# Another step order for the attention stage, and the range test of the softmax sums split in two

## The chip, the cores and the metric

The kernel runs on one core of a Trainium2 chip. The metric is device time in microseconds (us) of one execution; lower is better. Three runs of the kernel before gave 255.69, 255.74 and 256.41 us, median 255.74 us. The profile is one further execution, with a time of its own.

## The reference

Two branches work on the same 2048 x 512 input and are summed with it:

```python
xn = layernorm(x)                                  # 2048 tokens, 512 features
# A: 32 heads of width 16, causal window of 256 tokens
q, k, v = split(xn @ wqkv)
p = softmax(where(0 <= i - j < 256, q k^T / 4, -1e9))
A = (p v) @ wo
# B: gated MLP with spatial mixing
z = gelu(xn @ w_in)                                # 1376 wide, two halves of 688
g = w_sp @ layernorm(z[:, 688:]) + b_sp            # w_sp is 2048 x 2048
B = (z[:, :688] * g) @ w_out
out = x + A + B
```

All inputs and the output are bf16.

## The kernel before, in words

The kernel has a first stage (layernorm, `z`, most of q, k and v) and an attention stage, in which the attention, the spatial mixing and both output projections are interleaved. Nothing schedules at run time or at build time: every engine takes its instructions in the order in which the program issues them, and in the attention stage that order is the string `ORDER`, one token per step, read by the loop at the end of the kernel. A step issues work on several engines, so moving a step moves its work in all their queues.

The steps:

- `q4` and the numbers behind it: matmuls of 512 columns (L161) of the last four q/k/v projections; here they are tiles of v, which VectorE casts into `v_y` (L168).
- `S`: two score tiles. TensorE writes them into PSUM (`score_mm`, L761), ScalarE takes the exponential (L840), and GpSimd masks the window's edges with `affine_select` (L855) once both halves of a set are there. `B`, `A` and `T` are steps of three tiles, of which VectorE casts the third to bf16 (L838) ahead of its exponential; they also open (`B`, `T`) and close (`A`, `T`) an output tile `fo`.
- `D`: the corner blocks of a unit pair: 32 small score matmuls, two exponentials (L790). `d`: VectorE multiplies those with a mask (L862).
- `p`: the product with v of one of the 32 units (L727, 56 matmuls), followed on VectorE by the transposition `ot` (L734). `n`: VectorE normalizes one unit: a reciprocal into `r_all` (L740), a multiplication (`on`, L742) and a transposition (`oT`, L750).
- `g`: matmuls of 344 columns of the spatial mixing (L588), 16 to a tile `gf`; `g7 ... 9` is such a tile in two parts. VectorE then adds the bias and multiplies with `z1` into `u` (L602), and SyncE issues the transposing DMA of `u` and the load of a later `wspT`.
- `y`: matmuls of the output tile that is open (L662). `f`: those of an output tile on its own (L680, L687). At its end VectorE adds the input (`xo`, L627) and a DMA stores the result.

Two kinds of PSUM buffer couple the engines. The score tiles are three buffers (`ps_s`), so a score step waits until the exponentials of the tiles three earlier are through. All of `q`, `g`, `p`, `y` and `f` share two banks (`x_tile`), which alternate; while an output tile is open it holds one of them, and every `gf` takes the other.

The reciprocals of all softmax sums stay in `r_all`, 512 columns. After the last unit is normalized, `check_sums` tests them against a range with a `tensor_scalar` (L873) and a `scalar_tensor_tensor` with an accumulator (L874), and a DMA turns the 128 counts into one row (L879). Ahead of the last addition of `xo`, VectorE takes that row's minimum (`least_sum`, L886), then writes a flag (L892), which every engine loads; a slower path with a maximum follows only if a sum is out of range, which does not happen with these inputs.

Of the kernel before, what the change touches and what calls it, by code (L numbers as in the profile page):

```python
# [8 lines left out]
P = 128  # L9
BF = mybir.dt.bfloat16  # L10
F32 = mybir.dt.float32
ACT = mybir.ActivationFunctionType
ALU = mybir.AluOpType

S_TOK = 2048
D = 512
# [9 lines left out]
NG = 4  # L26
NJ = NB // 2
SM_SCALE = DH ** -0.5
LN_EPS = 1e-5
R_LOW = 2.0 ** -60  # L30
R_HIGH = 2.0 ** 40
# [11 lines left out]


ORDER = """
S q4 q2 S 2 q4 S q4 g7 D 9 S g10 S d 6 p S g5 n 11 D p p S p g7 D 5 n 3 d 1 g3 n 4 B y1 1 n y1 2
y1 3 y1 1 y1 2 A y3 g3 y1 5 d 2 B 5 y4 1 y2 A y1 g3 y1 2 y1 11 S p p D g12 S 4 n n g6 S 10 S p p
S g5 n 3 n 8 B y5 g1 y1 1 d y1 2 A 2 y1 5 y1 5 D p p D g4 n d 12 B n y2 g1 y1 1 y1 1 y1 3 A y1 1
y1 4 y1 1 y1 4 S p p S g8 n 6 d 2 B y4 g3 y1 1 n 3 A 1 y1 3 y3 5 D p p S g4 n 4 d 8 B y3 n g1 y1
3 y1 2 y1 A 1 y1 5 y2 4 D p p D g2 n 11 n 3 B y3 g3 d y1 1 y1 2 A 3 y2 1 y1 2 y1 4 S p p D g5 n  # L50
8 d 3 B y6 p A y2 d g11 y1 1 S 4 p n S p g6 n D 10 S p g6 n n 5 B y2 1 y1 3 y1 1 y1 d y4 T y8 n
y1 A g16 S p p D n g2 n 13 B y2 1 y4 d y3 T y9 A g16 D p p S g12 D d 4 g6 n S 8 n 2 S p p S g10
D n 4 n 2 f6 S 3 d 1 g7 S 9 S p p S g4 d 9 S n 3 g11 n 5 p p n f7 n 3 f10 f10 f10
"""


# [16 lines left out]
def kernel(  # L73
# [12 lines left out]
    nc = tc.nc  # L86
# [25 lines left out]
    r_all = pers.tile([P, NJ * NG, 16], F32, name="r_all")  # L112
# [63 lines left out]
    with ExitStack() as actx:  # L176
# [52 lines left out]
        for w in WARM:  # L229
# [11 lines left out]
            out=hmask[:],  # L241
# [4 lines left out]
        for m, off, old, new in ((maskY, 0, PAD, 0), (maskD, -PAD, 0, PAD)):  # L246
            nc.gpsimd.memset(m[:], 1.0)
            nc.gpsimd.affine_select(
                out=m[:, old : old + PAD], in_=m[:, old : old + PAD], pattern=[[-1, PAD]],
# [3 lines left out]
                out=m[:, new : new + PAD], in_=m[:, new : new + PAD], pattern=[[1, PAD]],  # L253
# [151 lines left out]
        def z_stats(n):  # L405
            if n % 2 == 0:
                zmv[n // 2] = sm.tile([P, 4, 2], F32, name="zmv")
            mvt = zmv[n // 2]
            st = sm.tile([P, 2, nc.vector.BN_STATS_DIM], F32, name="st2")
            for j in range(2):  # L410
                nc.vector.bn_stats(out=st[:, j, :], in_=z2n[:, n, j * HALF : (j + 1) * HALF])
            nc.vector.bn_aggr(out=mvt[:, n % 2, :], in_=st[:])
            if n % 2 == 1:
                return rstd(mvt, 2)
            return None
# [9 lines left out]
        for n in range(2):  # L425
# [6 lines left out]
            out=maskC[:, 0, :], in0=maskD[:, 0:PAD], in1=maskD[:, PAD:P], op=ALU.add  # L432
        )
        nc.vector.tensor_scalar(
            out=maskC[:, 1, :], in0=maskC[:, 0, :], scalar1=-1.0, scalar2=1.0,
            op0=ALU.mult, op1=ALU.add,
# [18 lines left out]
        for n in range(NB):  # L455
            b, j = divmod(n, 4)
# [25 lines left out]
            if n >= 1:  # L482
                r = z_stats(n - 1)
# [20 lines left out]
            if n % 2 == 1 and n >= 3:  # L504
                r = z_rs[n - 2]
# [4 lines left out]
            if n == NB - 1:  # L510
                r = z_stats(n)
# [11 lines left out]
    ep = ctx.enter_context(tc.tile_pool(name="ep", bufs=4))  # L523
# [6 lines left out]
    def late():  # L530
        if not late_pool:
            assert not work["q"]
            pq_ctx.close()
            late_pool.append(
                late_ctx.enter_context(tc.tile_pool(name="late", bufs=1, side="right"))
            )
            for i in range(2):
                vh = late_pool[0].tile([P, 4, VROW], BF, name=f"vh{i}")
                nc.gpsimd.memset(vh[PAD:P, 0:2, :], 0.0)
                nc.gpsimd.memset(vh[0:PAD, 2:4, :], 0.0)  # L540
                v_half.append(vh)
        return late_pool[0]
# [151 lines left out]
    E = {}  # L694
    ED = {}
    turned = {}
    later = []
# [39 lines left out]
    def normalize(J, G):  # L737
        ot = turned.pop((J, G))
        rsum = r_all[:, J * NG + G, :]
        nc.vector.reciprocal(out=rsum, in_=ot[:, :, DH])  # L740
        on = late().tile([P, 8, 32], BF, name="on", bufs=2)
        nc.vector.tensor_tensor(  # L742
            out=on[:].rearrange("p b (e d) -> p e b d", e=2),
            in0=ot[:].rearrange("p (e b) j -> p e b j", e=2)[:, :, :, 0:DH],
            in1=rsum.rearrange("p (e b) -> p e b", e=2).unsqueeze(3).to_broadcast([P, 2, 8, DH]),
            op=ALU.mult,
        )
        if G == 0:
            oTs[J] = late().tile([P, NC, 256], BF, name="oT", bufs=3)
        nc.vector.transpose(  # L750
            out=oTs[J][:, G, :], in_=on[:].rearrange("p b j -> p (b j)")
        )
# [55 lines left out]
    def do_slots(n, shut=False, open_=False):  # L808
        some = [slots.pop(0) for _ in range(n)]
        tiles = [ps_s.tile([P, 2, 512], F32, name="S", tag="S") for _ in range(n)]  # L810
        mms = []
        for (J, G, kind, h), S in zip(some, tiles):
            if kind == "P" and h == 0:
                E[(J, G)] = ep.tile([P, 8, 512], BF, name="E")
            if (J, G, kind, h) == (0, 2, "Q", 0):
                load_half(1)
            mms.append(list(slot_mms(J, G, kind, h, S)))
        if n == 3:
            h = some[1][3]
            score_mm(*mms[0].pop(0))  # L820
            if shut:
                rest_mm(half[0], 2 * h, False)
            if open_:
                new = half_open()
                rest_mm(new, 2 * h + 1, True)
            turns = [mms[0:1], mms[1:3]]
        else:
            turns = [mms]
        for turn in turns:
            for k in range(0, max(len(m) for m in turn), 2):  # L830
                for m in turn:
                    for args in m[k : k + 2]:
                        score_mm(*args)
        for i, ((J, G, kind, h), S) in enumerate(zip(some, tiles)):
            b0 = 4 * (kind == "Q") + 2 * h
            part, src = E[(J, G)][:, b0 : b0 + 2, :], S[:]
            if i == 2:
                nc.vector.tensor_copy(out=part, in_=src)  # L838
                src = part
            nc.scalar.activation(out=part, in_=src, func=ACT.Exp, scale=SM_SCALE)  # L840
            if h == 1:
                mask_set(J, G, kind)
        if shut:
            half_end()
# [15 lines left out]
    def mask_corners(J, G):  # L860
        v, mask = ED[(J, G // 2)][:], maskC[:, int(J == 0), :]
        nc.vector.tensor_tensor(  # L862
            out=v, in0=v, in1=mask.unsqueeze(1).to_broadcast([P, 32, PAD]), op=ALU.mult,
        )

    rows = []

    def check_sums():
        assert not (later or units)
        r = r_all[:].rearrange("p a b -> p (a b)")  # L870
        ok = ep.tile([P, 512], BF, name="ok", tag="E")
        low = ep.tile([P, 1], F32, name="low", tag="E")
        nc.vector.tensor_scalar(out=ok[:], in0=r, scalar1=R_LOW, scalar2=None, op0=ALU.is_ge)  # L873
        nc.vector.scalar_tensor_tensor(  # L874
            out=ok[:], in0=r, scalar=R_HIGH, in1=ok[:], op0=ALU.is_le, op1=ALU.mult,
            accum_out=low[:],
        )
        row = ep.tile([P, P], F32, name="row", tag="E")
        nc.sync.dma_start(out=row[0:1, :], in_=low[:])  # L879
        rows.append(row)  # L880
# [186 lines left out]
    units = [(J, G) for J in range(NJ) for G in range(NG)]  # L1067
# [6 lines left out]
    for step in ORDER.split():  # L1074
        if step in "STABCH":
            n = 2 if step == "S" else 1 if step == "H" else 3
            do_slots(n, step in "TA", step in "TB")
        elif step == "D":
            do_corners(*corners.pop(0))
        elif step == "d":  # L1080
            mask_corners(*masks.pop(0))
        elif step == "p":
            pv(*units.pop(0))
        elif step == "n":
            normalize(*later.pop(0))
        elif step[0] == "y":
            for _ in range(int(step[1:])):
                half_mm()
        else:
            if step[0] in work:  # L1090
                assert left == 0
                item = work[step[0]].pop(0)
                left, unit = (NFC + NC, f_work(*item)) if step[0] == "f" else item
                step = step[1:]
            for _ in range(int(step)):
                next(unit)
                left -= 1
            if left == 0:
                assert next(unit, None) is None
# [34 lines left out]
```

## Time and profile before

| | value |
|---|---|
| median of three runs | 255.74 us |
| profiled execution, time and span | 255.79 us, 254.0 us |
| first score matmul of the attention stage | 83.23 us |
| last matmul issued / last instruction on data | 250.21 us / 251.22 us |
| TensorE, VectorE, ScalarE, GpSimd busy | 97%, 79%, 77%, 41% of the span |

The span runs from the first to the last instruction of the trace; 1.8 us of the profiled execution's time lie outside it. Matmuls overlap in TensorE's pipeline, so their durations in the tables are longer than the time from one to the next: a matmul of 344 columns lasts 310 ns, and the next one starts 146 ns after it. The sums below therefore go by starts.

### The profile page before, as it was taken

Reading aid. Unit: us, or ns where it says so; the run is one execution under the profiler, and the core shown is the slowest. Engines: PE = TensorE matmul, PEld = TensorE weight load, DVE = VectorE, ACT = ScalarE, POOL = GpSimd, SP = SyncE. Lnnn points to the kernel's source line nnn. Section 1 sums busy time; section 2 is a strip of 40 time slices with the busy share of each in tenths; the row PEclk is TensorE's granted clock in tenths of the full one; section 3 lists DMA queues with packets and bytes.
Section 4 is the critical chain, followed back from the end, with each engine's and each line's share of the span. In section 5 each row is a group of like instructions: output and inputs, shape, how many; then the busy total and the mean of one; then the engine's idle time right before and its main releaser. Section 6 shows DMA issues by size and latency. Waiting matters only on the chain.

```text
span 254.0 us, 8684 instructions
## 1 busy us (share of the span) xinstructions
PE 247.7 (97%) x3712; PEld 141.3 (56%) x3712; DVE 200.1 (79%) x434; ACT 195.6 (77%) x234; POOL 105.3 (41%) x165
## 2 busy tenths in 40 slices
PE   7899999999999999999999999999999999999994
PEld 3555555555555356546557556566565464664653
DVE  7699977875657659985698898887998989684883
ACT  3756567556546998898989989889898899998900
POOL 3221211210010387575464465626484547543710
PEclk9999999999999999999999999999999999999999
DMA  6899722018400128646567717569184557675232
GB/s 198 291 252 195 195 54 31 1 41 104 105 1 0 44 46 122 143 124 137 54 86 181 131 44 189 50 157 157 38 168 41 138 77 126 117 101 125 36 54 69
DMA packets 67162, 26.82 MB, mean 106 GB/s; under 512 B 57040, under 2 KB 65584, under 8 KB 67120
## 3 DMA queue, kind: packets, MB, share of 16 engines
q1 hardware_dynamic: 66400, 25.50, 52.4%
q10 hardware_dynamic: 720, 0.73, 0.9%
q8 instruction: 30, 0.49, 0.9%
q14 instruction: 12, 0.10, 0.1%
HBM read 8.46 MB, written 2.10 MB: 42 GB/s over the span
## 4 chain that ended last, share of the span: by engine, by line
PE 92%; DMA 3%; DVE 2%; ACT 1%; issue 1%; SPq 0%; DVEq 0%
PE gf L588 31%; PE zp L370 14%; PE S L761 11%; PE fo L662 10%; PE o L727 9%; PE pj_o L143 6%; PE pj_f L143 5%; PE pj_o L161 3%; PE pj_f L161 2%; DMA w_in_sb<-in_B_w_in_dram 2%; DMA row<-low 1%; DVE xo L627 1%; PE fo L680 1%; PE zo L370 0%; PE fo L687 0%
## 5 line engine op out<-in xcount | busy, mean ns | idle before, releaser
L855 POOL TENSOR_SCALAR_AFFINE_SELECT E<-E 128x512 bf16<-128x512 bf16 x124 | 86.3, 721 | 68.0 <-ACT E L840 64.8
L840 ACT ACTIVATE E<-S 128x1024 bf16<-128x1024 f32 x102 | 97.6, 1027 | 9.1 <-PE S L761 9.0
L588 PE MATMUL gf<-z2n,wspT 128*128 128x344 bf16 x512 | 88.4, 310 | 0.0
L588 PEld LDWEIGHTS <-wspT 128*128 128x128 bf16 x512 | 47.4, 98 | 30.9 <-issue 5.9
L302 POOL TENSOR_TENSOR rs<-ve,mhalf 128x2 f32<-128x2 f32 (+1 forms) x18 | 12.1, 670 | 68.2 <-DVE ve L299 67.6
L370 PE MATMUL zp<-w_in_sb,xnT 128*128 128x344 bf16 x224 | 36.9, 309 | 0.1
L761 PE MATMUL S<-qpad,kT 32*64 32x128 bf16 (+2 forms) x848 | 32.0, 259 | 0.2 <-ACT E L840 0.2
L790 ACT ACTIVATE ED<-S 128x1024 bf16<-128x1024 f32 x30 | 29.1, 1024 | 1.6 <-PE S L761 1.5
L370 PEld LDWEIGHTS <-xnT 128*128 128x128 bf16 x224 | 21.6, 98 | 14.6 <-ACT xnT L361 0.7
L602 DVE SCALAR_TENSOR_TENSOR u<-gf,b_all,z 128x344 bf16<-128x344 f32 (+3 forms) x50 | 20.4, 438 | 11.7 <-PE gf L588 11.5
L734 DVE STREAM_TRANSPOSE ot<-o 128x512 f32<-128x512 f32 x32 | 22.5, 714 | 7.8 <-PE o L727 7.6
L838 DVE CAST E<-S 128x1024 bf16<-128x1024 f32 x22 | 26.7, 1213 | 2.2 <-PE S L761 2.2
L840 ACT ACTIVATE E<-E 128x1024 bf16<-128x1024 bf16 x22 | 23.4, 1063 | 0.8 <-DVE E L838 0.6
L727 PE MATMUL o<-E,v_y 128*32 128x128 bf16 (+1 forms) x736 | 23.5, 239 | 0.2
L761 PEld LDWEIGHTS <-kT 32*64 32x64 bf16 (+1 forms) x848 | 12.9, 99 | 18.6 <-issue 16.4
L727 PE MATMUL o<-ED,vh 128*32 128x64 bf16 x960 | 21.2, 193 | 0.0
L154 DVE TENSOR_SCALAR qpad<-qt,hmask 128x512 bf16<-128x512 bf16 x32 | 9.7, 348 | 13.6 <-ACT qt L152 13.6
L143 PEld LDWEIGHTS <-wqkv 128*128 128x128 bf16 x128 | 12.5, 98 | 12.8 <-DMA xnT<-xt 0.3
L862 DVE TENSOR_TENSOR ED<-ED,maskC 128x2048 bf16<-128x2048 bf16 x15 | 19.2, 1278 | 0.0
L378 ACT ACTIVATE z<-zp 128x688 bf16<-128x688 f32 x14 | 10.4, 743 | 10.9 <-PE zp L370 10.9
L143 PE MATMUL pj_o<-xnT,wqkv 128*128 128x512 bf16 x72 | 18.5, 379 | 0.0
L378 ACT ACTIVATE z2n<-zp 128x688 bf16<-128x688 f32 x14 | 10.4, 743 | 10.1 <-PE zp L370 10.1
(88 smaller groups left out, 306.7 us busy)
## 6 DMA issues: line engine op xcount, KB each, us to landing
vh<-v_y SPq DMA_DIRECT2D x16, 140.0 KB, 4.4
xo<-in_A_x_dram SPq DMA_DIRECT2D x16, 128.0 KB, 2.9
out_dram<-xo SPq DMA_DIRECT2D x15, 128.0 KB, 2.0
wqkv<-in_A_wqkv_dram SPq DMA_DIRECT2D x1, 1536.0 KB, 8.7
xt<-in_A_x_dram SPq DMA_DIRECT2D x2, 512.0 KB, 3.9
w_in_sb<-in_B_w_in_dram SPq DMA_DIRECT2D x5, 172.0 KB, 5.5
w_out_sb<-in_B_w_out_dram SPq DMA_DIRECT2D x1, 640.0 KB
w_in_sb<-in_B_w_in_dram ACTq DMA_DIRECT2D x3, 172.0 KB, 6.0
```

The costliest lines, as they stand in the source:

```text
L143: nc.tensor.matmul(pt[:], lhsT=wqkv[:, c, w0 : w0 + P], rhs=xnT[:, c, t0 : t0 + 512], start=(c == 0), stop=(c == NC - 1),)
L370: nc.tensor.matmul(out, lhsT=src[:, c, t0 : t0 + P], rhs=w_in_sb[:, c, f0 : f0 + HALF], start=(c == 0), stop=(c == NC - 1),)
L378: nc.scalar.activation(out=dst.rearrange("p (j f) -> p j f", j=2), in_=zp[:, :, 0:HALF], func=ACT.Gelu_apprx_tanh, scale=rsx[n] if n < 2 e ...
L588: nc.tensor.matmul(gf[:, 0:HALF], lhsT=wspT[t][:, c, :], rhs=z2n[:, c, j * HALF : (j + 1) * HALF], start=(c == 0), stop=(c == NB - 1),)
L662: nc.tensor.matmul(h["fo"][:], lhsT=lhsT, rhs=rhs, start=False, stop=(h["jobs"] == 2 and h["pos"] == NFH))
L727: nc.tensor.matmul(o[32 * s : 32 * s + 32, c0 + r0 : c0 + r0 + n], lhsT=v[:, m, h * VW : h * VW + 32], rhs=rhs(s), start=(i == 0), stop=(i ...
L734: nc.vector.transpose(out=ot[:].rearrange("p b j -> p (b j)"), in_=o[:])
L761: nc.tensor.matmul(out, lhsT=kT[32 * s : 32 * s + 32, g, k0 : k0 + nk], rhs=qpad[J // 2][32 * s : 32 * s + 32, g, :, qs - q00 : qs - q00 + ...
L790: nc.scalar.activation(out=Ed[:, 16 * i : 16 * i + 16, :], in_=S[i][:].rearrange("p b (x q) -> p (b x) q", q=PAD), func=ACT.Exp, scale=SM_ ...
L838: nc.vector.tensor_copy(out=part, in_=src)
L840: nc.scalar.activation(out=part, in_=src, func=ACT.Exp, scale=SM_SCALE)
L855: nc.gpsimd.affine_select(out=cells[:, :, k, :], in_=cells[:, :, k, :], pattern=pattern, compare_op=op, fill=0.0, base=base, channel_multi ...
```

## The change

`ORDER` is replaced. It has the same steps in the same numbers, plus one `c`; their places differ from the third token on. The new step `c` calls `test_sums`, which tests the part of `r_all` that has been normalized so far (28 units, 448 columns). `check_sums` tests the remaining four units (64 columns) at its old place, adds the two counts, and sends the sum by the same DMA. The limit that the flag compares with is the same.

```diff
 ORDER = """
-S q4 q2 S 2 q4 S q4 g7 D 9 S g10 S d 6 p S g5 n 11 D p p S p g7 D 5 n 3 d 1 g3 n 4 B y1 1 n y1 2
-y1 3 y1 1 y1 2 A y3 g3 y1 5 d 2 B 5 y4 1 y2 A y1 g3 y1 2 y1 11 S p p D g12 S 4 n n g6 S 10 S p p
-S g5 n 3 n 8 B y5 g1 y1 1 d y1 2 A 2 y1 5 y1 5 D p p D g4 n d 12 B n y2 g1 y1 1 y1 1 y1 3 A y1 1
-y1 4 y1 1 y1 4 S p p S g8 n 6 d 2 B y4 g3 y1 1 n 3 A 1 y1 3 y3 5 D p p S g4 n 4 d 8 B y3 n g1 y1
-3 y1 2 y1 A 1 y1 5 y2 4 D p p D g2 n 11 n 3 B y3 g3 d y1 1 y1 2 A 3 y2 1 y1 2 y1 4 S p p D g5 n
-8 d 3 B y6 p A y2 d g11 y1 1 S 4 p n S p g6 n D 10 S p g6 n n 5 B y2 1 y1 3 y1 1 y1 d y4 T y8 n
-y1 A g16 S p p D n g2 n 13 B y2 1 y4 d y3 T y9 A g16 D p p S g12 D d 4 g6 n S 8 n 2 S p p S g10
-D n 4 n 2 f6 S 3 d 1 g7 S 9 S p p S g4 d 9 S n 3 g11 n 5 p p n f7 n 3 f10 f10 f10
+S q4 q4 q1 S 3 q4 S g8 D 8 g2 S 4 d 6 S 4 p S g12 n 4 p D p n p D g8 n 1 S 7 g4 n 5 B 2 y1 3 y1
+2 y2 d y3 g3 A 4 y2 9 B y2 g1 y1 7 y1 A 2 y5 6 S p p D g4 d 1 n 6 S 5 g4 S 1 n 1 d 10 S p p S g2
+n 2 n 12 B y6 g3 y1 A 1 y1 8 y1 4 D p p D g6 n 4 d 6 B y3 g1 y2 n 2 y1 2 y1 A 1 y1 5 y1 5 S p p
+S g9 n 2 n 5 B y3 g1 d y1 1 y1 1 y1 1 A 1 y2 7 y1 4 D p p S g1 n 6 n 9 B y2 g3 d y1 1 y3 A 1 y1
+2 y2 9 D p p D g5 n 7 n 4 B y2 g6 d y4 A 2 y1 1 y1 3 y1 4 S p p D g5 d 1 n 10 B y6 p A y2 g8 y1
+3 S d 5 p S n p g3 n 4 D 9 S p d g9 n 3 B 3 y2 1 y4 n y3 T n y9 A g16 S p p D g3 n 8 n 4 B 1 y7
+d y2 T y9 A g16 D p p D g1 n 7 d 5 S 3 g4 d 3 S 8 n 1 S p p S n g11 S 5 g6 n c 4 D 6 f2 S 3 d 5
+S p p S g10 S 3 n 3 g11 n 5 p n p n f10 f10 f10 f10
 """
...
+    def test_sums():
+        n0, n1 = sum(tested), NJ * NG - len(units) - len(later)
+        r = r_all[:, n0:n1, :].rearrange("p a b -> p (a b)")
+        ok = late().tile([P, 512], BF, name="ok", tag="ot", bufs=3)
+        if not tested:
+            tested_sums.append(late().tile([P, 2], F32, name="ok_sums"))
+        nc.vector.tensor_scalar(
+            out=ok[:, 0 : r.shape[-1]], in0=r, scalar1=R_LOW, scalar2=None, op0=ALU.is_ge
+        )
+        nc.vector.scalar_tensor_tensor(
+            out=ok[:, 0 : r.shape[-1]], in0=r, scalar=R_HIGH, in1=ok[:, 0 : r.shape[-1]],
+            op0=ALU.is_le, op1=ALU.mult,
+            accum_out=tested_sums[0][:, len(tested) : len(tested) + 1],
+        )
+        tested.append(n1 - n0)
...
     def check_sums():
         assert not (later or units)
-        r = r_all[:].rearrange("p a b -> p (a b)")
...
+        test_sums()
+        sums = tested_sums[0]
+        low = late().tile([P, 1], F32, name="low_sum")
+        nc.vector.tensor_tensor(out=low[:], in0=sums[:, 0:1], in1=sums[:, 1:2], op=ALU.add)
         row = ep.tile([P, P], F32, name="row", tag="E")
         nc.sync.dma_start(out=row[0:1, :], in_=low[:])
         rows.append(row)
...
+        elif step == "c":
+            test_sums()
```

## Prediction

> **What bounds the kernel now.** I read the page first, then the waits, then the timeline of both ends of the attention stage.
>
> ```profile
> PE 247.7 (97%) x3712; PEld 141.3 (56%) x3712; DVE 200.1 (79%) x434; ACT 195.6 (77%) x234; POOL 105.3 (41%) x165
> PE 92%; DMA 3%; DVE 2%; ACT 1%; issue 1%; SPq 0%; DVEq 0%
> ```
>
> TensorE is busy all the time and carries 92% of the chain that ended last. The waits show who holds whom:
>
> ```profile
> PEld L761 <- issue: 16.4, 52, 0.5
> ACT E L840 <- PE S L761: 9.0, 15, 0.8
> PEld L727 <- DVE xo L627: 1.2, 4, 0.4
> PE S L761 <- ACT E L840: 0.2, 1, 0.2
> ```
>
> ScalarE waits 9.0 us for scores, TensorE waits hardly ever for exponentials. The 16.4 us are no wait for another engine: they lie where matmuls of another tile form begin. From starts in the timeline, a `g` matmul costs 0.146 us, a `q`, `y` or `f` 0.216, an `S` 0.33, a `B` or `A` 0.54, a `D` 0.36, a full `p` 0.68, and each change from 128-row matmuls to score or `p` steps about 0.10, always the same within 0.02. So the stage is this sum plus what TensorE waits. Both orders have the same steps and, counted in the strings, 139 changes of form: the sum, 165 us, does not move. Only the waits and the two ends can.
>
> The front, PE, ACT and DVE:
>
> ```profile
> 83.23 0.40 PE L761 MATMUL S<-qpad,kT 32*128 32x512 bf16 x4
> 83.56 1.47 PE L161 MATMUL pj_f<-wqkv,xnT 128*128 128x512 bf16 x6
> 84.96 0.39 PE L761 MATMUL S<-qpad,kT 32*128 32x512 bf16 x2
> 85.53 0.39 PE L761 MATMUL S<-qpad,kT 32*128 32x512 bf16 x2 [0.19 <-ACT E L840]
> 87.26 0.49 PE L761 MATMUL S<-qpad,kT 32*128 32x256 bf16 x8
> ...
> 83.07 1.28 ACT L516 ACT_TABLE_LOAD   x1
> 84.48 5.58 ACT L840 ACTIVATE E<-S 128x1024 bf16<-128x1024 f32 x6
> ...
> 84.75 0.69 DVE L168 CAST v_y<-pj_f 128x512 bf16<-128x512 f32 x1
> ```
>
> The second `S` is cut in two: its second tile needs the buffer of the first exponential, which starts only after the table load. TensorE stands 0.57 us (84.96 to 85.53). The third `S` takes 0.43 instead of 0.33, another 0.10.
>
> The end:
>
> ```profile
> 247.31 0.41 DVE L873 TENSOR_SCALAR ok<-r_all 128x512 bf16<-128x512 f32 x1
> 247.85 0.69 DVE L874 SCALAR_TENSOR_TENSOR ok<-r_all,ok 128x512 bf16<-128x512 f32 x1
> 248.72 0.53 SPq L879 DMA_DIRECT2D row<-low  x1
> 249.88 0.60 PE L687 MATMUL fo<-wo_sb,oT 128*128 128x256 bf16 x4
> 250.68 0.28 DVE L886 TENSOR_REDUCE low<-row 1x1 f32<-1x128 f32 x1 [0.83 <-DMA row<-low]
> 250.88 0.40 DVE L627 TENSOR_TENSOR xo<-fo,xo 128x256 bf16<-128x256 f32 x1
> 251.21 0.13 DVE L892 TENSOR_SCALAR flag<-low 1x1 int32<-1x1 f32 x1
> ```
>
> The last addition stands behind `least_sum`, which waits for the row's DMA (1.93 us after its issue). The last matmul ends at 250.48, and the addition could follow within 0.05 us, as the one before did (matmuls to 248.79 + 0.60 = 249.39, addition at 249.43). It starts at 250.88: 0.35 lost.
>
> **The front, step by step.** Nine `q` instead of six stand ahead of the second `S`. The third group of four `q` wants the bank that the first used, and VectorE empties that from 84.75 to 85.44, behind two normalizations; with 0.06 to release, 85.50. TensorE is there at 83.56 + 8 x 0.216 = 85.29: a new wait of 0.21. One `q` and a change of form later, 85.81, comes the second `S`; its buffer was free at 85.53. The third `S` comes at 85.81 + 0.33 + 7 x 0.216 + 0.10 = 87.75, its buffers free at 87.31. `D` comes at 87.75 + 0.33 + 8 x 0.146 + 0.10 = 89.35; its second buffer is that of the fifth exponential, 88.20 + 1.05 = 89.25: 0.10 to spare, and as little in the next three `S`. So 0.57 + 0.10 go and 0.21 comes: 0.46. What then becomes late is the third `p`. In the old order it reads its last mask at 99.12; the exponentials for it end at 97.63, GpSimd's two selections take 1.27, so that mask is ready at about 98.96. TensorE will be 0.4 earlier; the exponentials only 0.2 to 0.3, what ScalarE idles at 89.90 to 90.19. A wait between 0 and 0.23; I take 0.08, since the old margin was 0.16. Front: **0.38 gained**, between 0.15 and 0.53.
>
> A page speaks against this part. The Trainium skill, "ScalarE: Activation LUTs", section "What ACT_TABLE_LOAD costs", adds a drain of 1.38 us to a load of 1.28; by it, as an estimate, the first exponential would start so much later that the longer cover of nine `q` would not do either. The trace disagrees: the load takes 1.28, and the first exponential starts 0.13 after its end.
>
> **The middle.** The old order has three waits past 100 us, 0.26 in all; the longest, 0.16, is a `p` at 187.04 behind `xo`, itself behind a `d` of 1.68 us (184.71). The new order puts that `d` ahead of the block, so this one goes. New tight places: in `n 7 n 4 B y2 g6` and `n 2 n 5 B y3 g1` two `n` (1.09 each) are queued on VectorE shortly ahead of the emptying of `gf`, and while an output tile is open the next `gf` needs that very bank; I take 0.05 each, at most 0.4. In `3 d 5 S p p` the addition of `xo` is queued behind a `d` (1.18 to 1.68), and the second `p` needs its bank; 0.10, between 0 and 0.3. Middle: **0.05 gained**, between 0.85 lost and 0.26 gained. The step `c` costs VectorE at most 0.41 + 0.69 + 0.08; behind it is queued the emptying of a `gf` that ends ten `g` and a `D` later, 10 x 0.146 + 0.36 + 0.10 = 1.9 us, so I cost it at nothing (without that cover, up to 1.2). SyncE's queue moves along: a `wspT` lands 5.4 us after its issue, the issue comes 1.3 after that of `uT`, and its tile is two further on, 8 us later at the tightest place, early on, in either order; nothing there.
>
> **The end.** After the last `p` the new order has `n` ahead of it and only full `f` behind: the same matmuls in the same order. On VectorE `ot`, `n`, `ot`, `n` closes the gap of 0.22 ahead of the second `ot` (243.94), and the addition of the first `f` starts 0.30 earlier. The tests shrink from 512 to 64 columns. By rows of that size (a 48-column L602 0.26, a 16-column cast 0.17) I take 0.19 and 0.25 for 0.41 and 0.69, and the new addition of two counts costs 0.15 plus a wait of 0.1. The row is issued 0.30 + 0.22 + 0.44 - 0.25 = 0.7 us earlier and lands near 249.95; `least_sum` runs from 249.98 to 250.26, in VectorE's idle time ahead of the last addition. That then follows its matmuls at 250.53 instead of 250.88, and the flag, the last store and the closing semaphores follow it: **0.36 gained**. A landing up to 0.3 later still hides; past that the gain shrinks one for one.
>
> **Sum.** 255.79 (the profiled execution, span 254.0 and 1.8 around it) - 0.38 - 0.05 - 0.36 = 255.00. The median stands 0.05 below the profiled execution: **254.95 us**.
>
> **Rivals.**
>
> (1) TensorE's lead is handed back. ScalarE computes 150 of the 157 us between its first and last exponential, so a lead of 0.4 us may meet buffers and masks that are no earlier. For it: margins of 0.1 in the first ten steps. Against it: ScalarE's own waits for scores, 9 us, mean it is ahead for most of the stage. Only the end's gain is left: 255.74 - 0.36 = 255.4. Chance 0.2.
>
> (2) Slower: VectorE is late at the bank changes. In the blocks from `B` to `A` the new order often has two `y` between `B` and the next `gf`, where the old one had up to five. From the last `g` matmul to that `gf` TensorE needs 0.146 + 0.10 + 0.54 + 2 x 0.216 = 1.22; VectorE starts 0.36 after that matmul's start and needs 0.70 and 0.06 to release: 1.12. Whatever delays it more than 0.1 is a wait. A `d` took 1.68 instead of 1.18 while GpSimd selected, an `on` 1.54 instead of 0.43. The Trainium skill, "GPSIMD Engine Reference", section "Specifications", says that both engines share an interface to SBUF, with contention for instructions with two SBUF inputs; the two rows agree. Half a microsecond in each of five blocks is 2.5: 254.95 + 2.5 = 257.4. It decides from 0.3 a block on. Against it: the old order has the same lengthened rows and lost 0.26 by them. Chance 0.1.
>
> (3) More than that: the old middle waits go, no new ones come, the front keeps 0.53. 255.74 - 0.26 - 0.53 - 0.36 = 254.6. Chance 0.15.
>
> (4) The table load hides more than its row shows, and ScalarE starts later behind the new first steps, by as much as a load (1.28): the second `S` would wait for 86.82 instead of coming at 85.81, 255.95. This is the rule above as a mechanism; the trace shows 0.13, so 0.02.
>
> **How the numbers follow.** My forecast has 0.53. About 0.3% (0.77 us, below 254.97) is what a measurement can tell from no change; the forecast lies on that line. Faster: 0.35 of its 0.53 and all of (3), 0.50. Same: the rest of it, (1) and (4), 0.40. Slower: 0.10. The range takes in (3) below and (1) above with the middle's bounds: 254.4 to 255.6.
>
> **What would show it.** Right: the second `S` in one piece near 85.8 behind a `q` that starts at 85.5; the row's DMA 0.7 earlier against the last matmul, and no gap ahead of the last `xo`. Wrong: TensorE gaps ahead of `S`, `D` or the first four `p` (1), ahead of `gf` inside the blocks (2), or a first exponential later than 84.5 (4).

## The result, and the profile after

The changed kernel takes 257.0 us (median of 18 runs, 255.9 to 258.1) beside 255.79 for the kernel before on the same chip (18 runs, 255.03 to 256.44): ratio 1.0046, 95% interval 1.0033 to 1.0059. It is slower; the forecast of 254.95 and its range of 254.4 to 255.6 are missed. The profiled execution took 257.9 us, with a span of 256.1.

The page, engines and chain:

```profile
PE 247.4 (97%) x3691; PEld 141.3 (55%) x3712; DVE 203.0 (79%) x438; ACT 195.6 (76%) x234; POOL 107.0 (42%) x165
...
PE 91%; DVE 3%; ACT 2%; POOL 1%; issue 1%; POOLq 0%
```

TensorE's work is the same (21 matmul records are missing here), and its share of the chain is smaller. The waits say where:

```profile
PEld L761 <- issue: 16.5, 50, 0.6
...
ACT E L840 <- PE S L761: 9.6, 14, 1.3
...
PEld L727 <- DVE u L602: 1.8, 1, 1.8
PE o L727 <- DVE u L602: 1.7, 1, 1.7
```

A `p` waits once, 1.7 us, for an emptying of `gf` into `u`. No such row stood in the page of before. The front, TensorE:

```profile
85.46 0.40 PE L761 MATMUL S<-qpad,kT 32*128 32x512 bf16 x4
...
87.40 0.40 PE L761 MATMUL S<-qpad,kT 32*128 32x256 bf16 x8
...
89.00 0.43 PE L761 MATMUL S<-qpad,kT 32*64 32x128 bf16 x32
```

The second `S` is in one piece. The first `S` is at 82.88 here (83.23 before); second, third and `D` follow it by 2.58, 4.52 and 6.12, and the forecast said 2.58, 4.52 and 6.12. Then comes the first unit's `n`, and with it the loss:

```profile
95.52 3.88 POOL L855 TENSOR_SCALAR_AFFINE_SELECT E<-E 128x512 bf16<-128x512 bf16 x6
95.58 3.30 DVE L742 TENSOR_TENSOR on<-ot,r_all 128x256 bf16<-128x256 f32 x1
...
97.77 0.43 PE L761 MATMUL S<-qpad,kT 32*64 32x128 bf16 x32
...
98.92 0.45 DVE L750 STREAM_TRANSPOSE oT<-on 128x256 bf16<-128x256 bf16 x1
...
99.29 0.53 DVE L602 SCALAR_TENSOR_TENSOR u<-gf,b_all,z 128x344 bf16<-128x344 f32 x1
...
99.88 0.29 PE L727 MATMUL o<-E,v_y 128*32 128x256 bf16 x4 [1.68 <-DVE u L602]
```

Read it upwards from the last line. The third `p` wants the bank that `u` empties. `u` is queued on VectorE behind `oT` and `on` of the first unit, and that `on`, 0.42 to 0.43 where nothing disturbs it, takes 3.30 beside six selections on GpSimd. The same place in the kernel before:

```profile
95.80 3.88 POOL L855 TENSOR_SCALAR_AFFINE_SELECT E<-E 128x512 bf16<-128x512 bf16 x6
...
96.41 1.54 DVE L742 TENSOR_TENSOR on<-ot,r_all 128x256 bf16<-128x256 f32 x1
...
98.35 0.53 DVE L602 SCALAR_TENSOR_TENSOR u<-gf,b_all,z 128x344 bf16<-128x344 f32 x1
...
98.94 0.29 PE L727 MATMUL o<-E,v_y 128*32 128x256 bf16 x4
```

There `on` took 1.54 beside the same six selections (from 95.80), and the third `p` started at 98.94 without a wait, but also without any time to spare: `u` ended at 98.88, and from its end to the `p` there are 0.06, as in the changed kernel (99.82 and 99.88). What followed the wait in this execution of the changed kernel shows in windows of 1 us (the length of the window, busy time and instructions of PE, PEld, DVE, ACT and POOL, then PEclk, the granted clock, DMA share and GB/s):

```profile
102.00:103.00 1.00, 1.00 (x5) 0.54 (x4) 1.00 (x3) 1.00 (x2) 0.00 (x0) 0.50 1.09 227
106.00:107.00 1.00, 1.00 (x9) 0.61 (x7) 0.97 (x4) 0.74 (x1) 0.19 (x1) 1.00 0.00 0
```

From 101.48, for 3.41 us, the clock was 0.50 and a `g` took 0.287 us instead of 0.146. The end:

```profile
249.71 0.17 DVE L875 TENSOR_SCALAR ok<-r_all 128x64 bf16<-128x64 f32 x1
...
250.51 0.53 SPq L894 DMA_DIRECT2D row<-low_sum  x1
...
252.34 0.60 PE L687 MATMUL fo<-wo_sb,oT 128*128 128x256 bf16 x4
252.47 0.27 DVE L901 TENSOR_REDUCE low<-row 1x1 f32<-1x128 f32 x1 [0.16 <-DMA row<-low_sum]
252.98 0.42 DVE L627 TENSOR_TENSOR xo<-fo,xo 128x256 bf16<-128x256 f32 x1 [0.23 <-PE fo L687]
```

The reduction is done ahead of the last matmul's end, and the last addition starts 0.04 behind it (252.94). As forecast.

### The profile page after: what moved, and what is told of

It is laid out like the page before. It is cut to its first block, busy times and chain, and to the rows that moved or that the text cites. A ratio compares the mean times of both kernels' runs of the same rounds, so it can differ in the third digit from the quotient of the medians.

```text
span 256.1 us, 8662 instructions
## 1 busy us (share of the span) xinstructions
PE 247.4 (97%) x3691; PEld 141.3 (55%) x3712; DVE 203.0 (79%) x438; ACT 195.6 (76%) x234; POOL 107.0 (42%) x165
## 4 chain that ended last, share of the span: by engine, by line
PE 91%; DVE 3%; ACT 2%; POOL 1%; issue 1%; POOLq 0%
PE gf L588 30%; PE zp L370 14%; PE S L761 10%; PE fo L662 8%; PE o L727 8%; PE pj_o L143 6%; PE pj_f L143 5%; PE pj_f L161 3%; PE pj_o L161 3%; PE fo L680 2%; ACT E L840 1%; PE heat L230 1%; PE fo L687 1%; DVE on L742 1%; POOL E L855 1%
## 5 line engine op out<-in xcount | busy, mean ns | idle before, releaser
L855 POOL TENSOR_SCALAR_AFFINE_SELECT E<-E 128x512 bf16<-128x512 bf16 x124 | 87.8, 733 | 68.9 <-ACT E L840 65.6
L742 DVE TENSOR_TENSOR on<-ot,r_all 128x256 bf16<-128x256 f32 x32 | 19.1, 597 | 1.1
L727 PEld LDWEIGHTS <-v_y 128*32 128x32 bf16 x736 | 15.3, 97 | 6.3 <-issue 2.9
```

The source lines that it names most:

```text
L727: nc.tensor.matmul(o[32 * s : 32 * s + 32, c0 + r0 : c0 + r0 + n], lhsT=v[:, m, h * VW : h * VW + 32], rhs=rhs(s), start=(i == 0), stop=(i ...
L742: nc.vector.tensor_tensor(out=on[:].rearrange("p b (e d) -> p e b d", e=2), in0=ot[:].rearrange("p (e b) j -> p e b j", e=2)[:, :, :, 0:DH ...
L855: nc.gpsimd.affine_select(out=cells[:, :, k, :], in_=cells[:, :, k, :], pattern=pattern, compare_op=op, fill=0.0, base=base, channel_multi ...
```

## Experiments

Each ratio is to the kernel before, run on the same chip; its median was 255.69 to 255.88 in the four groups.

**Is the wait of the third `p` the loss?** The changed kernel again:

> The changed kernel once more, as the reference point for this set. All theories: about 257.0 us, ratio to the kernel before 1.003 to 1.006. Theory A (VectorE's first `on` collides with GpSimd's six selections in a row, the third `p` waits for a bank behind it, and TensorE's clock is halved for one stretch of 3.4 us after that wait in some executions): `on` of the first unit over 1.5 us, a wait of 0.5 to 1.7 us ahead of the third `p`, and a mean clock of 0.99 in about a third of the executions. Theory B (many small bank waits in the blocks from `B` to `A`): waits ahead of `gf` of 0.1 us and more, spread over the stage.

Measured: 256.51, ratio 1.0033 (1.0011 to 1.0055); `on` 3.31, the wait 1.7. Two of the 12 executions show a clock of 0.993, where about a third was expected. The profiled execution had a clock of 1.0 throughout and took 256.33, and none of its rows shows a wait of a `gf` matmul for another engine, so theory B has nothing to stand on.

The first `n` behind the third `p` instead of ahead of it, and the second behind the fourth (in each edit of the order the first line is the changed kernel's):

```diff
-S g12 n 4 p D p n p D g8 n 1 S
+S g12 4 p D p n p n D g8 n 1 S
```

> The changed kernel with the first two `n` one place later each: the first behind the third `p`, the second behind the fourth. Theory A: `on` starts after GpSimd's six selections are through, so 0.4 to 0.6 us instead of 3.3; no wait over 0.3 us ahead of the third `p`; mean clock 1.00 in every execution; 255.0 us, ratio to before 0.997. Theory B: no more than 0.2 us gained, ratio 1.003 to 1.005.

```profile
100.21 0.43 DVE L742 TENSOR_TENSOR on<-ot,r_all 128x256 bf16<-128x256 f32 x1
```

Measured: 255.37, ratio 0.9974 (0.9956 to 0.9993). `on` takes 0.43 at 100.21, and the third `p` stands some 0.4, by the starts of its matmuls, for a selection.

The zeros of `vh` written by VectorE, so that GpSimd is free for its selections as each pair of exponentials ends:

```diff
-                nc.gpsimd.memset(vh[PAD:P, 0:2, :], 0.0)
-                nc.gpsimd.memset(vh[0:PAD, 2:4, :], 0.0)
+                nc.vector.memset(vh[PAD:P, 0:2, :], 0.0)
+                nc.vector.memset(vh[0:PAD, 2:4, :], 0.0)
```

> The changed kernel with the four memsets of `vh` (1.03 us each on GpSimd) issued on VectorE instead. Theory A: GpSimd's selections run as soon as their exponentials are there, not six in a row, so `on` of the first unit takes at most 1.1 us and the third `p` waits less than 0.3 us; clock 1.00; 255.0 to 255.3 us, ratio 0.997 to 0.999. If the length of `on` has nothing to do with GpSimd: 3 us again, ratio 1.004. Theory B: ratio 1.003 to 1.005.

```profile
96.00 0.68 DVE L742 TENSOR_TENSOR on<-ot,r_all 128x256 bf16<-128x256 f32 x1
```

Measured: 255.11, ratio 0.9965 (0.9944 to 0.9985). The selections come in pairs at 93.92, 95.75 and 97.58; `on` takes 0.68, and there is no wait at the third `p`. Two different edits that have only the collision in common both turn the loss into a gain: the wait, with the halved clock that can follow it, is the loss. Both together:

> Both repairs in the changed kernel, the first two `n` one place later and the memsets of `vh` on VectorE. Theory A: what is left ahead of the third `p` after either repair is at most 0.36 us (the first) and 0 (the second), so the two together do not add up: 255.0 us, ratio 0.996 to 0.998. If each repair cured something of its own: 254.3 us, ratio 0.994.

Measured: 255.04, ratio 0.997 (0.9954 to 0.9987). They don't add up, as they should not if they cure one thing. This is the shortest median of all, 0.3% below the kernel before, though not to be told from the 255.11 of the memsets alone.

**Order and test apart.** The new order without `c`, all sums tested at the end as before:

> The new order without the split test: no `c`, the old check of 512 columns at its old place. All theories that take the end's gain as real: 0.36 us slower than the changed kernel, last addition again 0.3 to 0.4 us behind the last matmul, ratio to before 1.005 to 1.007. If the split test is what costs: ratio 1.000 or below.

Measured: 256.77, ratio 1.0039 (1.0013 to 1.0065), `on` 3.30, the last addition 0.34 behind the last matmul. The collision comes with the order alone. The 0.36 of the end show as 0.26 between medians (256.51); their intervals overlap, so by the times alone this difference isn't shown.

The old order with the split test:

```diff
-S p p S g4 d 9 S n 3
+S p p S g4 d c 9 S n 3
```

> The old order with the split test alone (`c` after the 28th `n`, the remaining four units tested at the old place). As predicted for the end: the last addition follows the last matmul by 0.05 us instead of 0.40, 0.36 us gained, 255.4 us, ratio 0.9985 to 0.9990. If `c` costs VectorE time that TensorE feels, or if something else ends the execution: ratio 1.000 or above.

Measured: 256.45, ratio 1.003 (1.0013 to 1.0046): a miss, though the last addition came right behind the last matmul. The timeline, VectorE and TensorE:

```profile
238.36 0.85 DVE L875 TENSOR_SCALAR ok<-r_all 128x448 bf16<-128x448 f32 x1
...
243.38 0.66 DVE L602 SCALAR_TENSOR_TENSOR u<-gf,b_all,z 128x296 bf16<-128x296 f32 x2
...
244.18 0.35 PE L727 MATMUL o<-E,v_y 128*32 128x256 bf16 x8 [1.32 <-DVE u L602]
```

`c` stands right behind a `d`, beside selections, takes 1.82 in all (0.85, 0.94 and the read of the count), and VectorE has no idle time until the last `u`, which the last `p` then waits for. So I had put it at a bad place. At a better one:

```diff
-f6 S 3 d 1 g7 S 9 S
+f6 S 3 d 1 c g7 S 9 S
```

> The old order, with the first test where VectorE is idle for some 2 us (behind the last d, ahead of g7 S 9 S). Theory: the end's gain is sound and only the place of c cost in the run before: last addition right behind the last matmul, no wait of 1.45 at the last p; 0.36 less than the kernel before, ratio near 0.9986. Rival (the split tests cost by themselves): a wait at a later p or f that VectorE releases, ratio near 1.003.

Measured: 255.09, ratio 0.9977 (0.9953 to 1.0002). `c` takes 1.04 from 231.79, in idle time; the last addition starts 0.04 behind the last matmul; the last `p` follows the one ahead of it as in the kernel before, by 0.29 from matmul to matmul (1.51 in the run above). That is the forecast's end, with no front. The interval takes in 1, so the trace shows this gain, and not the times.

**The clock behind the wait.** Does filling the wait keep the clock up?

```diff
-        for g in range(2):
+        for g in [0, 1] * (6 if (J, G) == (1, 0) else 1):
```

> The changed kernel with the 32 score matmuls of the second `D` issued six times, with the same values; the five repetitions take 5 x 0.26 to 0.36 us and lie where TensorE waits 1.7 us ahead of the third `p`. Theory A with the clock tied to TensorE's idle time: `on` takes 3.3 us as before, the wait shrinks to under 0.4 us, no execution with a mean clock under 0.995, 256.2 to 256.6 us. If the halved clock comes from something else: a clock of 0.99 in about one execution of five, as in the changed kernel.

Measured: 267.74, ratio 1.0474, and no answer. The 192 matmuls took 2.30 us and the third `p` did not wait for its bank, but inside it TensorE then stood 3.1 us with "issue" as releaser, and again 2.2 us up to 164.94 and 1.8 up to 230.53; behind the first two the clock was halved for 3.41. The filling made pauses of its own. The trace points at the loading of TensorE's program: loads of 16 KB of instructions start at 100.60, 162.17 and 227.78, beside the three pauses, and from one pause to the next TensorE issues 2304 and 2560 matmuls and weight loads, both multiples of 256. No run tested it.

And a longer wait (the first unit's transposition L750 five times)?

> The changed kernel with the transposition of the first unit's `n` issued five times on VectorE, 4 x 0.37 = 1.5 us more ahead of the emptying that the third `p` waits for. Theory A: the wait grows from 1.7 to 3.2 us, and with it the share of executions with a halved clock, from one in five to more than half; 258 to 259.5 us, ratio 1.009 to 1.014. If the wait had cover elsewhere: less than 0.5 us more than the changed kernel. If the clock has nothing to do with the wait: one execution in five as before.

Measured: 260.35, ratio 1.0174 (1.0147 to 1.02). The wait is 3.60. All 6 executions show a lower mean clock: 0.993 in three, which is one halved stretch of 3.41, and 0.985 in three, which is two. By the mean clock of each execution, over all runs but e6 (all six at 0.994 or lower):

| longest wait of a `p`, as its row shows it | kernels | executions at 0.993 or lower |
|---|---|---|
| at most 0.5 | before, e1, e2, e5, e8, e12, e13 | none |
| 1.3 | e4 | 0 of 12 |
| 1.6 to 1.7 | changed, e0, e3, e9, e10, e11 | 18 of 78 |
| 2.0 | e14 | 3 of 6 |
| 3.6 | e7 | 6 of 6 |

In these runs, the longer TensorE stood, the likelier the next 3.41 us ran at half speed. What that costs: in the changed kernel, the six executions with the lower clock have a median of 257.9, the other twelve 256.7; from the third `p` to the last matmul it took 152.79 in its profile and 151.23 in that of e0, whose clock stayed. In e14 the three with the lower clock are no longer than the other three, so there no cost shows.

**Why was `on` held for 3.30?** First theory: because it reads two operands from SBUF.

```diff
+        if (J, G) == (0, 0):
+            nc.vector.tensor_scalar(
...
+                scalar1=1.0, scalar2=None, op0=ALU.mult,
+            )
```

> The changed kernel with the first unit's on as a copy of one SBUF operand (it leaves out the division of that unit). Theory (the operation with two SBUF operands is what waits for the six selections in a row): that on takes 0.3 to 0.6 at 95.6, the emptying of u follows at about 97.5, the third p waits at most 0.4, ratio 0.997 to 0.999. Rival (any VectorE operation that reads SBUF is held): 3.3 us again, wait 1.7, ratio 1.0035.

```profile
95.26 3.31 DVE L743 TENSOR_SCALAR on<-ot 128x256 bf16<-128x256 f32 x1
```

Measured: 256.39, ratio 1.0022 (0.9997 to 1.0047); that copy of one operand took 3.31, and the wait was 1.57. The theory falls. With a running sum added to the same instruction (`op1=ALU.add, accum_out=...`):

> The changed kernel with the first unit's on as a one-operand copy that also sums its output (it leaves out the division of that unit). Theory (what is held is an operation that takes a second path into SBUF, by two operands or by a fast mode, and the summing form has no fast mode): on 0.4 to 0.9, the third p waits at most 0.5, ratio 0.997 to 0.999. Rival (every VectorE operation that reads f32 from SBUF is held): about 3.3, ratio 1.0035.

```profile
95.98 0.36 DVE L743 TENSOR_SCALAR_CACHE_REDUCE on<-ot 128x256 bf16<-128x256 f32 x1
```

Measured: 0.36 beside the same selections (from 96.04, back to back), the third `p` stands some 0.4, for a selection, 255.39, ratio 0.9976 (0.996 to 0.9992). So it isn't every f32 read either: what is held is the plain copy and the operation on two operands, and a summing copy or a transposition (0.445 to 0.448 beside selections or not) is not. The Trainium skill, "SBUF — State Buffer", section "Who interferes with whom", says that VectorE and GpSimd share one pair of SBUF ports, which locks one of them out: a VectorE operation with two SBUF inputs contends for it with a GpSimd instruction that reads SBUF, and so can `tensor_scalar` in a two-port mode, but not in the form that also writes out its accumulator. The two-operand rows, e9 and e13 agree. In the two-port case, it says, whoever issues first has the pair for the whole instruction; that a running GpSimd instruction could be followed by four more before VectorE's turn, it does not say. The whole instruction would be 0.65 here.

That was the open half: why five selections here and three in the kernel before? In both kernels the traces fit a reading: VectorE is let in behind the first selection whose next but one is not ready (in the changed kernel behind the fifth, as there is no seventh). Before, the third pair's exponential ended at 97.63, and the third selection at 97.68: if the release takes the 0.06 seen at the third `p`, too late to have the fifth selection ready, and `on` got in there. After, that exponential ended at 97.10 and the third selection at 97.40. By this a later exponential should shorten `on`:

```diff
+            if (J, G, kind, h) == (0, 2, "Q", 0):
+                nc.scalar.activation(out=part[:, 0:1, :], in_=src[:, 0:1, :], func=ACT.Exp, ...)
             nc.scalar.activation(out=part, in_=src, func=ACT.Exp, scale=SM_SCALE)
```

> The changed kernel with half an exponential of the set (0,2,Q) computed twice (ScalarE 0.5 us later there, in time that it idled from 97.10 to 98.29). Theory (VectorE gets in ahead of a selection only when no second selection behind it is ready): the third pair is no longer ready when the third selection ends at 97.4, so the first on ends behind the third, 2.1 us instead of 3.30, though ScalarE does more; the third p then waits for its last mask, near 99.5 instead of 99.88, 0.3 less than the changed kernel. Rival (six selections in a row always hold on until the fifth has ended, or a start early in the run does): 3.30 or more, and no gain.

```profile
95.04 3.88 POOL L857 TENSOR_SCALAR_AFFINE_SELECT E<-E 128x512 bf16<-128x512 bf16 x6
...
95.10 2.08 DVE L742 TENSOR_TENSOR on<-ot,r_all 128x256 bf16<-128x256 f32 x1
```

Measured: `on` 2.08, as said, beside six selections as close together as before; 255.22, ratio 0.9984 (0.9967 to 1.0001), 1.3 below the changed kernel's 256.51, where 0.3 was expected. The third `p` starts at 98.18; the wait left is 0.46, still for `u`, and not one up to 99.5 for a mask: that `p` needs the fifth selection only, which ended at 98.31. ScalarE does more, and the kernel is faster than the changed one. The other way, in the kernel before:

```diff
+            nc.gpsimd.memset(vh[0:PAD, 2, 0:128], 0.0)
```

> The kernel before, with one more GpSimd memset (128 columns, 0.2 us) behind the four of 1.03. Theory as in the run with the later exponential: the first selection starts at 96.05, so the third exponential pair (ready 97.69) is ready before the third selection ends (97.9), the first on (96.41) is let in only behind the fifth: 3.0 us instead of 1.54, its bank is emptied at 100.4, and the third p stands 1.3 to 1.5 us; ratio 1.005 to 1.007. Rival (length of the wait has another cause): on 1.3 to 1.8, ratio 1.0 to 1.001.

```profile
97.10 3.70 POOL L856 TENSOR_SCALAR_AFFINE_SELECT E<-E 128x512 bf16<-128x512 bf16 x6
...
97.47 3.61 DVE L743 TENSOR_TENSOR on<-ot,r_all 128x256 bf16<-128x256 f32 x1
...
102.07 0.29 PE L728 MATMUL o<-E,v_y 128*32 128x256 bf16 x4 [1.99 <-DVE u L603]
```

Measured: 258.74, ratio 1.0108 (1.0082 to 1.0134). With a memset of 0.2 us more, the kernel takes 3 us more: `on` goes from 1.54 to 3.61, and a halved clock comes in 3 of 6. Of the 3 us the wait explains 2.0; the profiled execution also had its first score matmul 1.06 later than before, ahead of anything the memset touches, and the rest isn't accounted for. The sign is as expected and the size is more: `on` got in behind the sixth selection, not the fifth. The memset of `u` that follows the selections directly may count as ready too; that wasn't tried.

**A repair that failed.** In the changed kernel a `p` near 190.5 waits some 0.3 for the second of two selections, of which a `d` stretches the first to 1.39. I put that `d` one `p` later (`S d 5 p S n p` to `S 5 p d S n p`), with the memsets on VectorE, and then with the first `n` later too:

> Memsets on VectorE, and the mask d ahead of the p near 188 put behind it. Theory: the wait of 0.32 for the selection that the d stretches goes, nothing comes: 0.3 less than with the memsets alone, near 254.8, ratio 0.9955. Rival: the d delays the emptying behind it by its 1.2 us and another p waits as much: ratio 0.9965 or above.

> The same with the first n later too. Theory: the two repairs at the third p do not add up, so no less than e10 by more than 0.1: near 254.7, ratio 0.9955. Rival: the first n still costs something ahead of the fourth p, and 0.3 more goes: 254.4, ratio 0.994.

Measured: 257.18, ratio 1.0054 (1.0025 to 1.0083), and 256.76, ratio 1.0045 (1.0018 to 1.0071). Both miss: the next `p` reads that very `ED`, and waits 1.73 for the `d` itself, which took 1.59 beside selections.

## Why the prediction was wrong, step by step

- **The front's first steps** hold to 0.01: stall of 0.57 gone, `q` wait 0.20 (forecast 0.21), third `S` undelayed, 0.46 gained up to `D`.
- **The third `p` is the step that failed.** The prediction took 0.08, bounded by 0.23, from its mask alone. That `p` also needs a bank, which VectorE empties behind the first `n`, and this wait was put at nothing without a look at the bank. In both orders that `n` starts as soon as the first `ot` is done, and TensorE has the same work from the first `p` to the third (16 `g`, an `S`, a `D` and a `p`); the rows of before, `u` to 98.88 and the `p` at 98.94, show no margin. The mask had hardly one either: the fourth selection took 0.83 beside `on`, the fifth ended at 99.07, not at the 98.96 of the prediction, and its matmuls began at 99.12; the margin of 0.16 was a misreading. The term was 1.7, some twenty times the value taken and seven times its bound. The row that would have priced it, `on` 1.54 beside six selections, was cited, but for the blocks between `B` and `A`; even priced at 1.54 it would have been short. Counted from the first score matmul, `on` started 0.48 earlier and the third pair's exponential ended 0.18 earlier than before, but the six selections began 0.06 later, behind four memsets of `vh` (1.03 each) on GpSimd. So when the third selection ended, the fifth was ready; e12 and e14 move that from either side, and `on` follows.
- **The halved clock** stands nowhere in the sum. It came in 6 of 18 executions, whose median is 1.2 above the others'. At full clock the sum is 0.46 and 0.36 gained, 1.7 lost, and nothing lost in the middle: 255.79 + 0.9, some 256.7; the twelve executions at full clock have a median of 256.7 (255.9 to 257.4).
- **The middle** came out at 0.04 gained (151.23 from the third `p` to the last matmul in e0, 151.27 before) where 0.05 was forecast, but in part by luck. Nothing waits ahead of `gf` in the blocks, so the 0.05 taken for each was too much, and at `3 d 5 S p p` (near 236 in e0) nothing waits either, where 0.10 was taken; the `p` near 190.5, which the sum doesn't have, waits some 0.3 for a selection. And a late third `p` gave the exponentials time: with the wait taken out by both repairs (e5) the same stretch takes 151.45. `c` took 1.46 (0.47, 0.94 and the read) instead of at most 1.18, with `u` right behind it, and nothing waited: costing it at nothing holds at this place. e4 shows its uncovered price, 1.2, as the prediction had it.
- **The end** holds: 0.36, in the changed kernel and alone in e8.
- **The rivals**: (2) had the kind of mechanism right (VectorE late at a bank because of GpSimd) and a time of 257.4, but at the wrong place, and with a chance of 0.1. Against it I had put that the old order lost only 0.26 by such rows; that was a property of the old order's spacing, not of the rows. (3) and (4) did not come: the first exponential started 0.12 behind the table load's end. A gap ahead of one of the first four `p` was named as the sign of (1), but it was VectorE's emptying that made it, and not ScalarE: (1) did not come in the changed kernel. Where the wait is taken out, a small part of it shows: in e5 the `D` and the `S` behind it wait some 0.1 each for exponentials.

With the collision taken out, by e1, e2 or e5, the ratios are 0.9974, 0.9965 and 0.997; the forecast's 255.0 to 255.79 is 0.9969. From the first score matmul to the last addition e5's profile takes 167.01, and before 167.65: 0.64 gained where the forecast had 0.79. So the rest of the sum was nearly right.

## What to carry to other kernels

An operation's place on its own queue is only half of its cost: ask also what the other engines will have ready beside it, because a VectorE operation that shares a path with GpSimd can wait for a whole run of GpSimd work. For each step that comes earlier, check every operand and every bank, not the one that was tightest before. And price a TensorE wait of some 1.6 us or more with the clock that may be lost behind it.

## What the runs showed of the hardware

- VectorE's `on` beside back-to-back selections of 0.65 took 1.54, 2.08, 3.30 or 3.61 instead of 0.43, according to how many selections were ready behind the running one; making ScalarE 0.5 us slower made it shorter. The rule of "next but one not ready" fits all of these but the last step of e14, and stays a reading of the traces.
- The granted clock was halved for 3.41 us behind waits of 1.6 to 1.7 us in 18 of 78 executions, and never behind 1.3 or less (12 executions at 1.3, all others at 0.5 or less). The Trainium skill, "TensorE: Matmul & The Clock Gate", Part 1, says that the clock is judged in free-running windows of 3413 ns and falls after an idle one; the length agrees, but here half a window of waiting was enough at times. Which executions are hit isn't settled: in e11's profile the wait of 1.73 lay within one window of that grid, and the clock stayed.
- After 160 additional small matmuls TensorE stood 3.1 us with nothing that the profile shows to wait for, and twice more later (e6). The pauses lie a multiple of 256 TensorE instructions apart and beside loads of 16 KB of instructions; that TensorE waited for these loads is a reading of this one trace.
